# Attention over channels, then a gated layer: tokens in chunks of 1024 with 512-column products

## The chip, the cores and the metric

The kernel runs on one core of one Trainium2 chip. The metric is the device time of one execution in microseconds (us). Three runs of the kernel before took 2254.05 to 2256.57 us, with a median of 2255.52 us.

## The reference

For each of 4 batches, `q`, `k` and `v` are 6080 tokens by 256 channels in float32. Columns are normalised over the tokens, a 256x256 softmax over channels is formed, and `v` times that goes through two projections with a gate between them.

```python
qn = q / (np.linalg.norm(q, axis=1, keepdims=True) + 1e-06)
kn = k / (np.linalg.norm(k, axis=1, keepdims=True) + 1e-06)
s = kn.transpose(0, 2, 1) @ qn / tau
s = s - s.max(-1, keepdims=True)
a = np.exp(s)
a /= a.sum(-1, keepdims=True) + 1e-09
x = (v @ a).reshape(24320, 256)          # 4 batches of 6080 tokens
h = x @ w_in                             # 256 -> 2048
g = h * (1.0 / (1.0 + np.exp(-1.702 * h)))
return g @ w_out                         # 2048 -> 256
```

## The kernel before, in words

The softmax matrix and `w_in` are multiplied into one 256x2048 weight for each batch, so that the hidden layer is one product of `v` with that weight. All operands of TensorE are split into a high part and the rest (`split`, lines 81 to 84: ACT casts the high part, DVE subtracts), and a product is three matmuls: high by high, high by rest, rest by high.

**Tiling.** The 16 slices of 128 hidden columns are taken in pairs (`fp`, 8 of them). A chunk is 512 tokens (line 65); a batch has 11 chunks of 512 and one of 448. For one chunk and one pair the work is a 2x2 block product (two slices, two halves of the tokens, and a contraction over two halves of the 256 channels), done with seven products in place of eight: sums of blocks of `v` (`v_sums`, POOL) and of the weight (`weight_sums`) are made beforehand, and sums of products afterwards. In the kernel before a token half is 256 columns (224 in the last chunk), so each of these 21 matmuls is 256 columns wide.

**One pair** (`Hidden`, lines 530 to 596). `begin` makes products 0 and 4, copies one to SBUF (ACT, line 561) and adds it to the other (DVE, line 562). `middle` makes two more with two DVE additions (lines 569 and 571). `end` makes three with two additions (lines 577 and 578); then `gate` runs twice, over 512 columns each: an activation on ACT (line 589), and the split into `gh` and `gl`. PSUM has eight banks: four in `ps_h` (two sets of `ps_x` and `ps_y`), two in `ps_o` for the sums of the second projection, and two in `ps_s` for the scores of the next batch.

**The second projection** (`project`, line 600) adds six matmuls of 512 columns (line 610) for each of the two slices to the two banks of the chunk. After slice 15 the banks are copied out (lines 618 and 620).

**Order.** TensorE's order is written by hand (line 770): `begin` of a pair, `end` of the one before, a projection, work beside it, `middle`, a projection, work beside it. There are 192 such half steps in a batch, and a table of them (`put`) says at which one the work beside is emitted: the loads of the next batch's `q` and `k` and their split (`prepare`), its scores (line 299: four matmuls of 512 columns for each two token tiles; line 308: four of 256), its norms and softmax, its weights, and the next chunk's `v` (`v_load`, `v_sums`, `v_split`). The other engines are ordered by a planner when the program is built; work marked `pinned` is issued after the newest copy of line 561. A tile whose pool has no free buffer waits for the last reader of an old one. In the first steps of batch 0 the weights still have to be converted from 64-bit words, and two chunks run in turns (line 777). From `WIDE` on, the buffers of that conversion serve as more room for `gh` and `gl` (line 591).

Of the kernel before, what the change touches and what calls it, by code (L numbers as in the profile page):

```python
# [27 lines left out]
def channel_attention_then_glu(  # L28
# [35 lines left out]
    RT = 4  # L64
    chunks = [(o, min(NCH, N - o)) for o in range(0, N, NCH)]
    NCHUNK = len(chunks)

    const = ctx.enter_context(tc.tile_pool(name="const", bufs=1))
# [87 lines left out]
    def win_convert(n):  # L156
        g, c = divmod(n, NC2)
        if g not in win:
            win[g] = sp.tile([P, NC2, GW], F32, tag="win", name="win", bufs=1)
        yield from to_float32(win[g][:, c, :], words.pop(("in", n)), [P, GW])  # L160
# [17 lines left out]
    class Attention:  # L178
        def __init__(self, b, direct=0):
            self.b = b  # L180

            self.direct = direct
            self.alone = b == 0
            self.raw = {}
            self.firsts = {}

            short = UT if self.alone else 0
            self.rt = 6 if self.alone else RT
            self.loads = [(t, self.rt) for t in range(short, T + 1, self.rt)]
            if short:  # L190
                self.loads.insert(0, (0, short))
            self.wh = [None] * NG
            self.wl = [None] * NG

            self.units = [(t, min(UT, T - t)) for t in range(0, T, UT)]
            if TAIL:
                self.units.append((T, 1))

        def load(self, t0, room):
# [5 lines left out]
            tiles = {}  # L205
            for a, z in zip(cuts, cuts[1:]):
                for src, tag in ((q, "raw_q"), (k, "raw_k")):
                    if tag not in tiles:
                        if self.alone:
                            n = (t0 + self.rt - 1) // self.rt % NG  # L210
                            as_tag = {"raw_q": "wh", "raw_k": "wl"}[tag] + str(n)
                            tiles[tag] = wp.tile([P, self.rt, C], F32, tag=as_tag, name=tag)
                        else:
# [42 lines left out]

        def score_first(self, n):


            ps = ps_o.tile([P, NCH], F32, tag="o", name="s_first")  # L260
            todo = [(u, j, i) for u in range(self.direct) for j in range(UT) for i in range(NC2)]
            for m, (u, j, i) in enumerate(todo):
                rq, rk = self.fetched(u)
                nc.tensor.matmul(
                    ps[:, i * C : (i + 1) * C],
                    lhsT=rk[:, j, i * P : (i + 1) * P],
                    rhs=rq[:, j, :],
                    start=m == 0, stop=m == len(todo) - 1,
                    skip_group_check=True,
                )  # L270
# [3 lines left out]
            self.x = small.tile([P, NC2, C], F32, tag="x", name="x")  # L274
            nc.scalar.copy(self.x, ps.rearrange("p (c x) -> p c x", c=NC2))

        def score(self, u, qs, ks):
            nt = self.units[u][1]
            start = 0 if self.alone else self.direct
            if u == start:  # L280
                self.s = [
                    ps_s.tile([P, 2 * C], F32, tag=f"s{i}", name=f"s{i}")
                    for i in range(NC2)
                ]
            steps = [(j, i) for j in range(nt) for i in range(NC2)]
            last = u == len(self.units) - 1
            if u < self.direct:
                for j, i in steps:
                    nc.tensor.matmul(  # L289
                        self.s[i][:, :C],  # L290
                        lhsT=ks[:, j, i * P : (i + 1) * P],
                        rhs=qs[:, j, :],
                        start=u == start and j == 0,
                        stop=last and j == nt - 1,
                    )
                return

            for j, i in steps:
                nc.tensor.matmul(  # L299
                    self.s[i],  # L300
                    lhsT=ks[:, j, 0, i * P : (i + 1) * P],
                    rhs=qs[:, j, :, :],
                    start=u == start and j == 0,
                    stop=False,
                    skip_group_check=True,
                )
            for j, i in steps:
                nc.tensor.matmul(  # L308
                    self.s[i][:, C:],
                    lhsT=ks[:, j, 1, i * P : (i + 1) * P],  # L310
                    rhs=qs[:, j, 0, :],
                    start=False,
                    stop=last and j == nt - 1,
                    skip_group_check=True,
                )

        def norms_a(self, meanwhile=None):

            assert UT == 2
            ps = ps_h.tile([P, NCH], F32, tag="h", name="ps_n")  # L320
# [26 lines left out]
        def norms_c(self):  # L347

            ps = ps_h.tile([P, NCH], F32, tag="h", name="ps_b")
# [8 lines left out]
        def softmax_a(self, meanwhile=None):  # L358
            begun = not self.alone and self.direct
            if not begun:  # L360
                self.x = small.tile([P, NC2, C], F32, tag="x", name="x")
            self.z = small.tile([P, NC2], F32, tag="z", name="z")
            m = small.tile([P, NC2], F32, tag="m", name="m")
            for i in range(NC2):
                x, z, mi = self.x[:, i, :], self.z[:, i : i + 1], m[:, i : i + 1]
                s = self.s[i][:, :C]
                if not self.alone:
                    if begun:
                        nc.vector.tensor_tensor(x, self.s[i][:, C:], x, op=ALU.add)
                    else:  # L370
                        nc.scalar.copy(x, self.s[i][:, C:])
                    nc.vector.tensor_tensor(x, s, x, op=ALU.add)
                    s = x
                nc.vector.scalar_tensor_tensor(
                    x, in0=s, scalar=self.rn[:, NC2 + i : NC2 + i + 1], in1=self.rq,
# [24 lines left out]
        def spare(self, i, name):  # L400

            if self.alone:
                return ps_h.tile([P, NCH], F32, tag="h", name=name)
            return ps_s.tile([P, NCH], F32, tag=f"s{i}", name=name)

        def transposes(self, meanwhile=None):
            self.aT_h = small.tile([P, NC2, C], F32R, tag="aT_h", name="aT_h")
            self.aT_l = small.tile([P, NC2, C], F32R, tag="aT_l", name="aT_l")
            ps = self.spare(0, "ps_t")
# [12 lines left out]
        def win_load(self, g):  # L422

            win[g] = sp.tile([P, NC2, GW], F32, tag="win", name="win", bufs=1)
            nc.sync.dma_start(win[g], parts[g])

        def win_split(self, g, step=split):
            self.win_h = sp.tile([P, NC2, GW], F32R, tag="qs", name="win_h")
            self.win_l = sp.tile([P, NC2, GW], F32R, tag="ks", name="win_l")
            if self.alone:  # L430
                parts[g] = dram.tile([P, NC2, GW], F32, name=f"win{g}")
                nc.sync.dma_start(parts[g], win[g])
            return step(self.win_h, self.win_l, win[g])

        def weights(self, g, i):
# [7 lines left out]
            ps = self.spare(i, "ps_w")  # L443
# [14 lines left out]
            for f in range(2):  # L458
                nc.scalar.copy(self.wf[0][:, ((0, 3), (1, 2))[i][f]], src[:, f])  # L459
# [27 lines left out]
    def v_load(b, c):  # L487
# [3 lines left out]
        hw = w // 2  # L491

        early = b == 0 and c < 2
        room = [(wp, f"{t}{1 + c}") if early else (cv, "words") for t in ("wh", "wl")]
        t, u = (
            pool.tile([P, n, NCH // 2], F32, tag=tag, name="v_raw")
            for n, (pool, tag) in zip((4, 3), room)
        )
        vraw[b, c] = (t, u)
        src = vT[b, :, o : o + w].rearrange("(c p) (h n) -> p c h n", p=P, h=2)  # L500
        nc.sync.dma_start(t[:, 1:3, :hw], src[:, 1])
        nc.sync.dma_start(t[:, 0, :hw], src[:, 0, 0])
        nc.sync.dma_start(t[:, 3, :hw], src[:, 0, 1])

    def v_sums(b, c):

        hw = chunks[c][1] // 2
        t, u = (x[:, :, :hw] for x in vraw[b, c])
        eng = nc.gpsimd
        eng.tensor_tensor(u[:, 1], t[:, 2], t[:, 3], op=ALU.subtract)  # L510
        eng.tensor_tensor(t[:, 3], t[:, 3], t[:, 0], op=ALU.subtract)
        eng.tensor_tensor(u[:, 0], t[:, 2], t[:, 3], op=ALU.subtract)
        eng.tensor_tensor(u[:, 2], t[:, 1], u[:, 0], op=ALU.subtract)

    def v_split(b, c, part, step=split):

        hw = chunks[c][1] // 2
        if part == 0:
            vparts[b, c] = [
                vp.tile([P, 7, NCH // 2], F32R, tag=t, name=t) for t in ("vh", "vl")  # L520
            ]
        n = 4 if b == 0 and c < 2 else 2
        o = slice(2 * part, min(2 * part + n, 7))
        i = slice(2 * part % 4, 2 * part % 4 + (o.stop - o.start))
        h, l = (x[:, o, :hw] for x in vparts[b, c])
        return step(h, l, vraw[b, c][part // 2][:, i, :hw])

    wide = [0]

    class Hidden:  # L530
# [3 lines left out]
        def __init__(self, at, b, c, fp):  # L534
# [3 lines left out]
            self.v = vparts[b, c]  # L538

        def product(self, out, wi, vi, first=False, last=False):  # L540
            (wh, wl), (vh, vl) = self.w, self.v
            for n, (l, r) in enumerate(((wh, vh), (wh, vl), (wl, vh))):
                nc.tensor.matmul(  # L543
                    out, lhsT=l[:, wi, :], rhs=r[:, vi, : self.hw],
                    start=first and n == 0, stop=last and n == 2,
# [3 lines left out]
        def begin(self):  # L549
            hw = self.hw  # L550
            x, y = (ps_h.tile([P, NCH], F32, tag="h", name=nm) for nm in ("ps_x", "ps_y"))
            self.x = x[:, : 2 * hw].rearrange("p (h n) -> p h n", h=2)
            self.y = y[:, : 2 * hw].rearrange("p (h n) -> p h n", h=2)
# [338 lines left out]
```

## Time and profile before

| | |
|---|---|
| three runs, median (lowest to highest) | 2255.52 us (2254.05 to 2256.57) |
| profiled execution, first to last instruction (span) | 2252.1 us |
| TensorE (PE) busy, of the span | 2226.4 us, 99% |
| VectorE (DVE) busy | 1685.4 us, 75% |
| ScalarE (ACT) busy | 1339.5 us, 59% |
| GpSimd (POOL) busy | 446.3 us, 20% |
| mean granted TensorE clock | 0.999 |
| the chain that ended last | PE 91%, DVE 5%, ACT 2% |

Matmuls are pipelined, so the record of one lasts longer than the time until the next can start. What a matmul takes of TensorE's time is read from the starts of consecutive rows of the timeline.

### The profile page before, as it was taken

The page shows a single profiled execution, that of the slowest core. Times are in us where ns is not written, and L with a number is a line of the kernel's source. Part 1 is how long each engine was busy: PE and PEld are TensorE (multiplying, and loading weights), DVE is VectorE, ACT ScalarE, POOL GpSimd, SP SyncE. Part 2 cuts the span into 40 slices and gives each one's busy share as a digit, 9 for nine tenths or more (in the row PEclk, how much of TensorE's full clock was granted, in tenths as well). Part 3 has the DMA queues.
Part 4 walks back from the last instruction along what each step waited for, and adds up shares of the span by engine and source line. Part 5 has one row for each costly group of instructions (what it writes and reads, how often), then busy time and mean ns, then how long its engine had stood idle before and what let it go on. Part 6 is the DMA issues. An engine that isn't in the chain of part 4 may idle for free.

```text
span 2252.1 us, 36953 instructions
## 1 busy us (share of the span) xinstructions
PE 2226.4 (99%) x13712; PEld 1999.4 (89%) x13712; DVE 1685.4 (75%) x3346; ACT 1339.5 (59%) x2714; POOL 446.3 (20%) x420
## 2 busy tenths in 40 slices
PE   9899999999999999999999999999999999999999
PEld 8678888889989898988989999998898999999998
DVE  7988888776777878876677877877667666666665
ACT  7676666555666666655565666665556555555554
POOL 1024332210122323320022233331012101001000
PEclk9999999999999999999999999999999999999999
DMA  9222222100111212110010212110001000000000
GB/s 339 98 85 76 66 68 62 48 20 28 48 37 57 66 57 81 59 38 29 28 48 28 66 57 84 57 36 29 20 28 47 28 29 20 29 29 20 29 18 19
DMA packets 55205, 118.78 MB, mean 53 GB/s; under 512 B 6128, under 2 KB 20976, under 8 KB 55024
## 3 DMA queue, kind: packets, MB, share of 16 engines
q1 hardware_dynamic: 55024, 116.42, 15.9%
q8 instruction: 107, 1.75, 0.3%
q14 instruction: 74, 0.61, 0.1%
HBM read 89.39 MB, written 27.00 MB: 52 GB/s over the span
## 4 chain that ended last, share of the span: by engine, by line
PE 91%; DVE 5%; ACT 2%; issue 1%; DMA 1%; SPq 0%; DVEq 0%; ACTq 0%
PE ps_o L610 44%; PE ps_x L543 23%; PE ps_y L543 17%; PE s L299 3%; PE ps_w L452 2%; PE s L308 1%; PE s L289 1%; DVE wl L83 1%; DVE gl L83 0%; DVE win_l L83 0%; DVE u L562 0%; DMA raw_k<-in_k 0%; DVE z L133 0%; ACT wf L459 0%; DMA words<-in_w_in 0%
## 5 line engine op out<-in xcount | busy, mean ns | idle before, releaser
L83 DVE TENSOR_TENSOR gl<-g,gh 128x512 fp32r<-128x512 f32 (+1 forms) x768 | 568.8, 750 | 243.9 <-ACT gh L82 241.8
L610 PE MATMUL ps_o<-gl,wo_h 128*128 128x512 f32 (+1 forms) x1536 | 603.3, 393 | 0.9 <-DVE gl L83 0.9
L610 PE MATMUL ps_o<-gh,wo_h 128*128 128x512 f32 (+1 forms) x1536 | 604.2, 393 | 0.0
L610 PE MATMUL ps_o<-gh,wo_l 128*128 128x512 f32 (+1 forms) x1536 | 594.8, 387 | 0.0
L589 ACT ACTIVATE g<-ps_x 128x512 f32<-128x512 f32 (+1 forms) x384 | 227.2, 592 | 370.0 <-DVE ps_x L577 365.8
L82 ACT CAST gh<-g 128x512 fp32r<-128x512 f32 (+1 forms) x768 | 436.8, 623 | 1.0
L543 PE MATMUL ps_x<-vh,wh 128*128 128x256 f32 (+1 forms) x1536 | 433.3, 282 | 1.1 <-DVE r L569 1.1
L543 PE MATMUL ps_x<-vh,wl 128*128 128x256 f32 (+1 forms) x1536 | 433.8, 282 | 0.0
L543 PE MATMUL ps_x<-vl,wh 128*128 128x256 f32 (+1 forms) x1536 | 433.7, 282 | 0.0
L561 ACT COPY r<-ps_x 128x256 f32<-128x256 f32 (+1 forms) x384 | 142.7, 372 | 414.5 <-PE ps_x L543 414.3
L610 PEld LDWEIGHTS ps_o<-gh,wo_l 128*128 128x128 f32 x1536 | 288.7, 188 | 62.5
L543 PE MATMUL ps_y<-vh,wh 128*128 128x256 f32 (+1 forms) x1152 | 327.9, 285 | 12.3 <-DVE u L562 6.2
L543 PE MATMUL ps_y<-vh,wl 128*128 128x256 f32 (+1 forms) x1152 | 325.7, 283 | 1.9 <-DVE wl L83 1.9
L543 PE MATMUL ps_y<-vl,wh 128*128 128x256 f32 (+1 forms) x1152 | 325.3, 282 | 0.0
L610 PEld LDWEIGHTS ps_o<-gh,wo_h 128*128 128x128 f32 x1536 | 291.5, 190 | 34.6
L610 PEld LDWEIGHTS ps_o<-gl,wo_h 128*128 128x128 f32 x1536 | 291.5, 190 | 31.5 <-DVE gl L83 1.8
L543 PEld LDWEIGHTS ps_x<-vh,wh 128*128 128x128 f32 x1536 | 293.5, 191 | 16.2 <-DVE r L569 1.9
L543 PEld LDWEIGHTS ps_x<-vl,wh 128*128 128x128 f32 x1536 | 293.6, 191 | 12.5
L543 PEld LDWEIGHTS ps_x<-vh,wl 128*128 128x128 f32 x1536 | 293.8, 191 | 0.2 <-DVE wl L83 0.2
L562 DVE TENSOR_TENSOR u<-ps_y,r 128x256 f32<-128x256 f32 (+1 forms) x384 | 160.8, 419 | 139.0 <-ACT r L561 129.8
L543 PEld LDWEIGHTS ps_y<-vh,wh 128*128 128x128 f32 x1152 | 219.7, 191 | 36.1 <-DVE u L562 12.1
L569 DVE TENSOR_TENSOR r<-ps_x,u 128x256 f32<-128x256 f32 (+1 forms) x384 | 159.6, 416 | 121.4 <-PE ps_x L543 121.4
(119 smaller groups left out, 2991.2 us busy)
## 6 DMA issues: line engine op xcount, KB each, us to landing
out_T<-osb SPq DMA_DIRECT2D x88, 256.0 KB, 2.3
raw_q<-in_q SPq DMA_DIRECT2D x33, 512.0 KB, 3.6
raw_k<-in_k SPq DMA_DIRECT2D x33, 512.0 KB, 4.5
v_raw<-in_vT SPq DMA_DIRECT2D x44, 256.0 KB, 2.8
v_raw<-in_vT SPq DMA_DIRECT2D x88, 128.0 KB, 2.9
win<-win SPq DMA_DIRECT2D x16, 512.0 KB, 3.2
raw_q<-in_q SPq DMA_DIRECT2D x6, 768.0 KB, 8.9
raw_k<-in_k SPq DMA_DIRECT2D x6, 768.0 KB, 10.2
```

What stands on the lines that cost most here:

```text
L82: ins = nc.scalar.copy(dst_hi, src)
L83: nc.vector.tensor_tensor(dst_lo, src, dst_hi.bitcast(F32), op=ALU.subtract)
L289: nc.tensor.matmul(self.s[i][:, :C], lhsT=ks[:, j, i * P : (i + 1) * P], rhs=qs[:, j, :], start=u == start and j == 0, stop=last and j == ...
L299: nc.tensor.matmul(self.s[i], lhsT=ks[:, j, 0, i * P : (i + 1) * P], rhs=qs[:, j, :, :], start=u == start and j == 0, stop=False, skip_gro ...
L308: nc.tensor.matmul(self.s[i][:, C:], lhsT=ks[:, j, 1, i * P : (i + 1) * P], rhs=qs[:, j, 0, :], start=False, stop=last and j == nt - 1, sk ...
L452: nc.tensor.matmul(ps, lhsT=l[:, j, ci], rhs=r[:, j, :], start=n == 0, stop=n == 3 * NC2 - 1,)
L543: nc.tensor.matmul(out, lhsT=l[:, wi, :], rhs=r[:, vi, : self.hw], start=first and n == 0, stop=last and n == 2, skip_group_check=True,)
L561: newest[0] = nc.scalar.copy(r1, self.x[:, 0])
L562: nc.vector.tensor_tensor(u2, self.y[:, 1], r1, op=ALU.add)
L569: nc.vector.tensor_tensor(r, self.x[:, 1], self.u2, op=ALU.add)
L589: nc.scalar.activation(g, ps, AF.Gelu_apprx_sigmoid)
L610: nc.tensor.matmul(out[d][:, :w], lhsT=l[:, f, ds], rhs=r[:, :w], start=f == 0 and n == 0, stop=f == NF - 1 and n == 2,)
```

## The change

A chunk becomes 1024 tokens, and a half of it 512 columns (the last chunk of a batch has 960, so 480), in the same seven products. One pair now takes three banks (`a`, `b`, `c`, each single), the second projection four (`o0` to `o3`, two for each half), and the scores one (`s`). A pair is four steps (`slot` 0 to 3), with one projection of the pair in step 3 and the other three in steps 0 to 2 of the next pair. There are again 192 steps in a batch. Three results are copied from PSUM to SBUF by ACT and three DVE additions follow; one of the four gated blocks is gated in SBUF. The pair of buffers for `gh` and `gl` goes from three to two, with two more from `WIDE` on. Scores of the next batch go into one bank, by three matmuls of 256 columns where there was one of 512 and one of 256. The split `w_in` is kept in DRAM in both parts and loaded again, where it was split again. `q` and `k` of a later batch are loaded two token tiles at a time (before: four).

```diff
-    chunks = [(o, min(NCH, N - o)) for o in range(0, N, NCH)]
+    WCH = 2 * NCH
+    chunks = [(o, min(WCH, N - o)) for o in range(0, N, WCH)]
-    vp = ctx.enter_context(tc.tile_pool(name="vp", bufs=2))
-    gp = ctx.enter_context(tc.tile_pool(name="gp", bufs=3))
+    vp = ctx.enter_context(tc.tile_pool(name="vp", bufs=1))
+    gp = ctx.enter_context(tc.tile_pool(name="gp", bufs=2))
-    ps_h = ctx.enter_context(tc.tile_pool(name="ps_h", bufs=4, space=PSUM))
-    ps_o = ctx.enter_context(tc.tile_pool(name="ps_o", bufs=2, space=PSUM))
+    ps_h = ctx.enter_context(tc.tile_pool(name="ps_h", bufs=1, space=PSUM))
+    ps_o = ctx.enter_context(tc.tile_pool(name="ps_o", bufs=1, space=PSUM))
+    def bank(tag, name):
+        pool = {"a": ps_h, "b": ps_h, "c": ps_h, "s": ps_s}.get(tag, ps_o)
+        return pool.tile([P, NCH], F32, tag=tag, name=name)
...
             for j, i in steps:
+                ci = slice(i * P, (i + 1) * P)
+                self.product(i, ks[:, j, 0, ci], qs[:, j, 0, :])
+                self.product(i, ks[:, j, 0, ci], qs[:, j, 1, :])
+                self.product(i, ks[:, j, 1, ci], qs[:, j, 0, :], last and j == nt - 1)
...
         def win_load(self, g):
-            win[g] = sp.tile([P, NC2, GW], F32, tag="win", name="win", bufs=1)
-            nc.sync.dma_start(win[g], parts[g])
+            for t, part in zip((self.win_h, self.win_l), parts[g]):
+                nc.sync.dma_start(t.bitcast(F32), part)
...
+    V_ROOM = {"px": (2, 2), "py": (2, 2), "pz": (2, 1), "pw": (1, 1)}
...
+        def copied(self, src):
+            r = gp.tile([P, NCH], F32, tag="r", name="r", bufs=3)[:, : self.hw]
+            newest[0] = nc.scalar.copy(r, src)
+            return r
+
+        def slot(self, k):
             hw = self.hw
+            if k == 0:
+                self.z = bank("c", "ps_z")[:, :hw]
+                self.product(self.z, 3, 3, first=True)
+                self.r5 = self.copied(self.z)
+                self.x = bank("a", "ps_x")[:, :hw]
+                self.product(self.x, 0, 0, first=True)
+                r1 = self.copied(self.x)
+                y = bank("b", "ps_y")[:, :hw]
+                self.product(y, 1, 1, first=True, last=True)
+                nc.vector.tensor_tensor(y, y, r1, op=ALU.add)
+                self.gate(0, 0, y)
+            elif k == 1:
+                self.product(self.x, 4, 4)
+                self.r2 = self.copied(self.x)
+            elif k == 2:
+                self.product(self.x, 5, 5)
+                nc.vector.tensor_tensor(self.r5, self.x, self.r5, op=ALU.add)
+                self.product(self.z, 6, 2, last=True)
+                nc.vector.tensor_tensor(self.z, self.z, self.r2, op=ALU.add)
+                self.gate(0, 1, self.z)
+                self.gate(1, 1, self.r5)
+            else:
+                self.product(self.x, 2, 6, last=True)
+                self.gate(1, 0, self.x)
...
-            there = wide[0] and wide[0] % 5 < 2
+            there = wide[0] and gates[0] % 2
+            gates[0] += 1
             pool, tags = (cv, ("z", "low")) if there else (gp, ("gh", "gl"))
...
-                    at_u = first + 4 * (u - nd)
+                    at_u = first + 5 * (u - nd)
                     put(at_u - 4, nxt.fetched, u)
                     put(at_u, pinned, prep, u)
                     put(at_u + 3, score, u)
-                e = first + 4 + 4 * (nu - nd)
+                e = between(first + 4 + 5 * (nu - nd))
                 put(e, nxt.norms_a)
-                put(e + 9, nxt.norms_c)
-                put(e + 10, nxt.softmax_a)
-                put(e + 16, nxt.transposes)
+                put(e + 4, nxt.norms_c)
+                put(e + 5, nxt.softmax_a)
+                put(e + 8, nxt.transposes)
...
+            for s in range(total):
+                at_slot = s % SLOTS
+                if at_slot == 0:
+                    h = Hidden(at, b, *divmod(s // SLOTS, NF // 2))
+                h.slot(at_slot)
+                if at_slot == 3:
+                    h.project(0, 0)
+                elif before is not None:
+                    before.project(*((0, 1), (1, 0), (1, 1))[at_slot])
+                for fn, a in side.get(s, ()):
+                    fn(*a)
+                if at_slot == 3:
+                    before = h
```

## Rows read from the trace of the kernel before

**Rows 1.** The profile's page: span, and busy time of each engine (part 1).

```profile
span 2252.1 us, 36953 instructions
...
PE 2226.4 (99%) x13712; PEld 1999.4 (89%) x13712; DVE 1685.4 (75%) x3346; ACT 1339.5 (59%) x2714; POOL 446.3 (20%) x420
```

**Rows 2.** Busy time by stretch: from:to, length, then each engine's busy us.

```profile
0.00:180.00 180.00, 161.59 (x858) 138.17 (x859) 153.87 (x289) 126.77 (x234) 40.11 (x45) 0.99 0.48 169
...
1800.00:2252.00 452.00, 448.14 (x2817) 405.94 (x2815) 298.66 (x647) 233.63 (x477) 29.32 (x36) 1.00 0.07 24
```

**Rows 3.** TensorE's waits after 180 us: releaser, total us, times, longest; the largest.

```profile
PE ps_y L543 <- DVE u L562: 1.8, 10, 0.2
```

**Rows 4.** TensorE's waits before 180 us: the one with the longest single wait.

```profile
PE ps_y L543 <- DVE u L562: 4.4, 2, 3.0
```

**Rows 5.** Timeline of TensorE in batch 1: start, record's length, line, tiles, shape.

```profile
799.80 0.28 PE L543 MATMUL ps_x<-vh,wh 128*128 128x256 f32 x1
...
801.60 0.40 PE L610 MATMUL ps_o<-gh,wo_h 128*128 128x512 f32 x1
801.83 0.40 PE L610 MATMUL ps_o<-gl,wo_h 128*128 128x512 f32 x1
802.07 0.39 PE L610 MATMUL ps_o<-gh,wo_l 128*128 128x512 f32 x1
...
802.99 0.28 PE L543 MATMUL ps_y<-vh,wh 128*128 128x256 f32 x1
...
803.70 0.40 PE L610 MATMUL ps_o<-gh,wo_h 128*128 128x512 f32 x1
```

**Rows 6.** The same view: the scores of two token tiles, and what follows.

```profile
840.92 1.07 PE L299 MATMUL s<-qs,ks 128*128 128x512 f32 x4
841.83 0.64 PE L308 MATMUL s<-qs,ks 128*128 128x256 f32 x4
842.30 0.28 PE L543 MATMUL ps_x<-vh,wh 128*128 128x256 f32 x1
```

**Rows 7.** The same view in the last chunk: a projection of 448 columns, products of 224.

```profile
2215.11 0.37 PE L610 MATMUL ps_o<-gh,wo_h 128*128 128x448 f32 x1
...
2216.33 0.27 PE L543 MATMUL ps_y<-vh,wh 128*128 128x224 f32 x1
...
2216.99 0.38 PE L610 MATMUL ps_o<-gh,wo_h 128*128 128x448 f32 x1
```

**Rows 8.** Groups by shape: one part of the products into `ps_x`; count, busy us, mean ns.

```profile
L543 PE MATMUL ps_x<-vh,wh 128*128 128x256 f32 x1408 | 398.6, 283 | 1.1 <-DVE r L569 1.1
```

**Rows 9.** Groups by shape on ACT and DVE: count, busy us, mean ns of one.

```profile
L83 DVE TENSOR_TENSOR gl<-g,gh 128x512 fp32r<-128x512 f32 x704 | 527.2, 758 | 220.3 <-ACT gh L82 218.5
L82 ACT CAST gh<-g 128x512 fp32r<-128x512 f32 x704 | 403.4, 627 | 0.8
...
L589 ACT ACTIVATE g<-ps_y 128x512 f32<-128x512 f32 x352 | 208.7, 593 | 1.5 <-DVE ps_y L578 1.5
L577 DVE TENSOR_TENSOR ps_x<-ps_x,u 128x256 f32<-128x256 f32 x352 | 150.2, 427 | 19.5 <-PE ps_x L543 16.4
...
L561 ACT COPY r<-ps_x 128x256 f32<-128x256 f32 x352 | 131.4, 373 | 395.3 <-PE ps_x L543 395.3
...
L83 DVE TENSOR_TENSOR ks<-raw_k,ks 128x512 fp32r<-128x512 f32 x65 | 106.4, 1637 | 0.0
...
L618 DVE COPY osb<-ps_o 128x512 f32<-128x512 f32 x44 | 30.1, 683 | 0.0
...
L620 ACT COPY osb<-ps_o 128x512 f32<-128x512 f32 x44 | 25.8, 587 | 54.4 <-PE ps_o L610 54.4
```

**Rows 10.** Timeline of ACT around one softmax: table load, and the next copy.

```profile
474.83 1.28 ACT L388 ACT_TABLE_LOAD   x1
...
479.68 0.35 ACT L561 COPY r<-ps_x 128x256 f32<-128x256 f32 x1
```

**Rows 11.** The profile's page: loads of `k`, KB each, median us to landing.

```profile
raw_k<-in_k SPq DMA_DIRECT2D x33, 512.0 KB, 4.5
```

More of the change, by code (lines that the diff above doesn't have):

```diff
@@ L188, in __init__ @@
             self.rt = 6 if self.alone else RT
-            self.loads = [(t, self.rt) for t in range(short, T + 1, self.rt)]
+            self.early = ["px", "py"][: direct * UT // 4] if not self.alone else []
+            begun = short + 4 * len(self.early)
+            self.loads = [(4 * n, 4) for n in range(len(self.early))]
+            self.loads += [(t, self.rt) for t in range(begun, T + 1, self.rt)]
             if short:
@@ L273, in score_first @@
             yield
-            self.x = small.tile([P, NC2, C], F32, tag="x", name="x")
-            nc.scalar.copy(self.x, ps.rearrange("p (c x) -> p c x", c=NC2))
         def score(self, u, qs, ks):
             nt = self.units[u][1]
[L279 to L284, printed above, removed]
+            if u == 0:
+                self.start_scores("o3" if self.alone else "s")
             steps = [(j, i) for j in range(nt) for i in range(NC2)]
@@ L288, in score @@
                 for j, i in steps:
[L289 to L294, printed above, removed]
+                    self.product(
+                        i, ks[:, j, i * P : (i + 1) * P], qs[:, j, :], last and j == nt - 1
                     )
@@ L298, in score @@
             for j, i in steps:
[L299 to L315, printed above, removed]
+                ci = slice(i * P, (i + 1) * P)
+                self.product(i, ks[:, j, 0, ci], qs[:, j, 0, :])
+                self.product(i, ks[:, j, 0, ci], qs[:, j, 1, :])
+                self.product(i, ks[:, j, 1, ci], qs[:, j, 0, :], last and j == nt - 1)
         def norms_a(self, meanwhile=None):
             assert UT == 2
[L320 removed]
+            ps = bank("b", "ps_n")
             for n in range(2 * NC2):
@@ L347, in norms_c @@
         def norms_c(self):
-            ps = ps_h.tile([P, NCH], F32, tag="h", name="ps_b")
+            ps = bank("c" if self.alone else "b", "ps_b")
             for i in range(NC2):
@@ L442, in weights @@
                 ]
-            ps = self.spare(i, "ps_w")
+            ps = bank("ac"[i] if self.alone and g == 0 else "b", "ps_w")
             ci = slice(i * P, (i + 1) * P)
@@ L505, in v_sums @@
[L505 to L526, printed above, removed]
@@ L530, in channel_attention_then_glu, with v_split @@
+    def v_split(b, c, tag, step=split):
+        hw = chunks[c][1] // 2
+        n, bufs = V_ROOM[tag]
+        h, l = (
+            vp.tile([P, n, NCH], F32R, tag=f"{tag}_{t}", name=f"v{t}", bufs=bufs) for t in "hl"
+        )
+        vparts[b, c, tag] = h, l
+        x, y = vraw[b, c, tag in ("pz", "pw")]
+        src = {"px": x, "py": y, "pz": y, "pw": x[:, 1:, :]}[tag]
+        return step(h[:, :, :hw], l[:, :, :hw], src[:, :, :hw])
+    wide = [False]
+    gates = [0]
     class Hidden:
```

328 lines of the change are left out of this document (149 added, 179 removed).

## The prediction

> **What bounds the kernel now.** I read the busy times of the page first, then the stretches, then TensorE's waits, and last its timeline. TensorE is busy for 2226.4 of 2252.1 us, no other engine for more than 1685.4 [rows 1]. Of the 25.7 us in which it is idle, 18.4 lie in the first 180 us [rows 2]; after that its largest wait sums to 1.8 us in ten pieces [rows 3]. So behind the start the kernel is one row of matmuls without gaps, and only what a matmul takes of TensorE's time, and the number of matmuls, set the end. Busy time doesn't tell that: the record of a 256-column matmul lasts 0.28 us and of a 512-column one 0.40, and they overlap [rows 5]. The starts tell it. Fifteen matmuls of 256 columns run from 799.80 to 801.60, six more from 802.99 to 803.70: 21 in 2.51 us, 0.1195 each. Six of 512 columns run from 801.60 to 802.99: 0.2317 each [rows 5]. Two of 256 take 0.239, one of 512 takes 0.2317: twice the width costs less than twice the time.
>
> **The products.** Before, a pair of slices of one chunk has 21 product matmuls. 4 batches x 12 chunks x 8 pairs x 21 = 8064, of which 32 x 21 = 672 are in the last chunks and 7392 are 256 wide (the group of 1408 is one of the three parts of the four products into one tile: 11 chunks x 8 x 4 x 4) [rows 8]. In the last chunks six of 224 columns run from 2216.33 to 2216.99, 0.110 each, and six of 448 from 2215.11 to 2216.33, 0.2033 each [rows 7]. Sum: 7392 x 0.1195 + 672 x 0.110 = 957.2 us. After, there are 4 x 6 x 8 x 21 = 4032, 3360 of 512 columns and 672 of 480. No 512-wide product is in the trace. The nearest rows are the projections: the same three matmuls (the first two with one weight, the streamed operand changing from high part to rest and back), 0.2317. At 480 columns I go halfway between 0.2033 and 0.2317, 0.2175. Sum: 3360 x 0.2317 + 672 x 0.2175 = 924.7, a gain of **32.5 us**. The bounds: the scores' four matmuls of 512 take 0.91 us, 0.2275 each [rows 6], where one streamed operand serves two weights; with that (0.2133 at 480) the gain is 49.5. The longest interval among the projections is 0.24, from 801.83 to 802.07 [rows 5]; if every product took that (0.2258 at 480), the sum would be 958.1 and the gain nothing. I take the projections' mean because the operands follow each other in the same way.
>
> **The projections** keep their six matmuls per slice and half. Before, 4224 of them are 512 wide and 384 are 448 wide: 978.7 + 78.1 = 1056.8 us; after, 3840 and 768 of 480: 889.7 + 167.0 = 1056.7. Nothing.
>
> **The scores.** Before, four of 512 in 0.91 us and four of 256 in 0.47 [rows 6] for two token tiles. After, twelve of 256: 12 x 0.1175 = 1.41, or 1.43 at the products' 0.1195. That is 0.03 to 0.05 us more for each of 68 such units (272 matmuls of line 299 in all, four to a unit): **+3 us**, on the path, since TensorE has no gaps.
>
> **ACT and DVE.** For 1024 tokens and one pair ACT loses two copies of 256 columns (0.373) and gains three of 512 from PSUM (0.587, the copy of line 620): +1.0 us x 192 = +195 on 1339.5, near 68% of the span. DVE loses ten additions of 256 (0.427) and gets three of 512 (0.683, the copy of line 618, is the nearest row): -2.2 x 192 = -425 on 1685.4 [rows 1, 9]. Neither engine becomes the bound; both costs are hidden by TensorE as long as no chain through them is longer than TensorE's way round. The work that `w_in`'s second split took from both goes as well.
>
> **The chains in a pair, with single banks.** A product takes 0.70 us and a projection 1.39, a pair 45 x 0.2317 = 10.43. From the start of step 0: z to 0.70, x to 1.39, y to 2.09, projection to 3.48, x again to 4.17, projection to 5.56, x again to 6.26, z again to 6.95, projection to 8.34, x a last time to 9.04, projection to 10.43. A result is there about 0.2 us later (a record of 0.39 against an interval of 0.23, and the next engine). Three waits are new. (1) Step 2 adds to x, so the copy r2 has to be done: 4.37 + 0.59 = 4.96 against 5.56, a margin of 0.6. (2) Step 3 adds to x, so DVE's r5 has to be done: 6.46 + 0.69 = 7.15 against 8.34, a margin of 1.2. (3) The next pair starts bank `a` at 11.13, so the activation of x has to be done. ACT gets z at 7.15 + 0.69 = 7.84; two activations (0.593) and two casts (0.627), whose starts are about 0.5 apart, end at 9.9; the activation of x ends at 10.5: a margin of 0.6. Behind a late r2 on ACT stand the gate of z and r5, and behind TensorE's wait for it everything else, the projections too. Work beside the pair can take the margins: on DVE one subtraction for `ks` lasts 1.64 us on average [rows 9], 0.4 more than margin (2); on ACT a softmax with its table loads keeps the copy waiting from 474.83 to 479.68 [rows 10], 4.85 us with two casts among them, three times. I count up to 3 us for each softmax, and 0.1 us for about half of the 140 pairs that have work beside them: 0 to 25 us, of which I take **+10**.
>
> **The start.** TensorE's longest wait in the early part, 3.0 us for DVE's addition of line 562 [rows 4], goes: the same bank's next product now waits for a copy on ACT alone, which doesn't stand behind DVE's weight splits. DVE, busy for 153.9 of 180 us there [rows 2], gets 2.2 us of each 10 back. Against that, `gh` and `gl` have two pairs of buffers for the 6.5 pairs until `WIDE`: the cast of x must wait for the projection of z (3.48), and cast 0.63, subtraction 0.76 and two handovers end at 5.1 where its own projection would start at 4.17, 0.9 us a pair. What is late next is y's projection. -8 to +12, taken as **0**.
>
> **Queues.** SP issues two loads of `w_in` parts per weight group in place of one and loads of `q` and `k` twice as often, half as large; each stands four or more steps of 2.6 us ahead of its use, and a 512 KB load lands in 4.5 us [rows 11]. POOL's sums take as many elements as before. I cost these at nothing; the cover gone, each late load stops the row of matmuls for what it lacks.
>
> **The sum.** On the profiled execution: 2252.1 - 32.5 + 3 + 10 + 0 = 2232.6; the median lies 3.4 us above that execution's span, which I keep: **2236 us**. Its own range: best 49.5 gained, 3 paid, no stalls and 8 saved at the start, near 2201; worst 32.5 gained with 25 of stalls, 2251. I call 2207 to 2251 its range.
>
> **The rivals.** (A) The single banks cost more than the width gives. For: three banks where two sets of two stood, margins of 0.6 us, and ACT 9 points busier, in strict order. Against: DVE has 20 points less to do, and the trace shows no waits with DVE at 75%. The price: if the 140 pairs with work beside lose the 0.44 us by which a `ks` subtraction overruns margin (2), 62 us in place of 10, 2288 us. It turns to slower where stalls pass 30 us, 0.16 us a pair of all 192. (B) The start: two pairs of buffers cost 0.9 us for x and as much for y over 6.5 pairs, 12 us, 2248. (C) The width gives next to nothing, because the part of a matmul beyond its columns isn't one per instruction but grows with the width: it is 0.24 for some projections, and at that price for all products the time is 2236 + 32.5 = 2268; at 0.2365 about 2256. For it speaks that the projections' intervals are uneven, 0.23 and 0.24 [rows 5], with the same order of operands; against it that the mean over six is 0.2317. The Trainium skill's page "TensorE: Matmul & The Clock Gate", section "Wait — 56ns, not 53.3ns?", puts that fixed part at about 2.5 ns for each matmul and the whole of a 512-column one at 215.7 ns, by which halving 4032 pairs of matmuls would save only 10 us, and C would hold. The trace does not agree: two of 256 less one of 512 is 7 to 11 ns by its rows.
>
> **How the numbers follow.** Forecast 0.58; A 0.17; B 0.13; C 0.10; 0.02 that stalls at the start vanish and products run at the scores' pace, below 2207. A measurement can tell about 0.2%, 4.5 us, so the bounds are 2251 and 2260. The forecast is faster; B is 0.11 faster and 0.02 within; C 0.01 faster, 0.05 within, 0.04 slower; A 0.01 within and 0.16 slower. Faster 0.72, same 0.08, slower 0.20. The range 2207 to 2266 leaves out most of A and the low tail.
>
> **What would show it.** In the trace after: six 512-column product matmuls from start to start in 1.39 us (1.365 is the better bound, 1.44 is C); TensorE's matmul rows fewer by about 3760 (4032 products less, 272 scores more); ACT near 68% busy, DVE near 56%. Waits of products into ps_x for ACT's copy r or its g above 30 us in sum are A; waits of line 610's successor for gl before about 140 us are B. The forecast goes wrong above all if ACT's order, made by the planner from its own times, puts work beside ahead of r2 or of the gate of x.

## The result, and the profile after

| | before | changed |
|---|---|---|
| median | 2255.38 us | 2230.68 us |
| lowest to highest of four runs | 2254.05 to 2256.57 | 2229.19 to 2231.76 |
| ratio of the changed kernel to the one before, 95% interval | | 0.9892 (0.9878 to 0.9906) |
| profiled execution's span | 2252.1 us | 2228.8 us |

The change gained 24.7 us, 1.1%; 19.5 were forecast. That the sum came out near is luck: the matmuls gained more than forecast and the stalls cost more, by some 30 us each.

The page of the changed kernel, span and busy times (part 1), against [rows 1]:

```profile
span 2228.8 us, 27422 instructions
...
PE 2174.7 (98%) x9952; PEld 1806.7 (81%) x9952; DVE 1321.5 (59%) x1894; ACT 1568.5 (70%) x2769; POOL 428.8 (19%) x348
```

TensorE's records are 3760 fewer, 13712 to 9952, the number forecast. ACT is at 70% and DVE at 59%, near the 68 and 56 that were worked out. TensorE's idle time has doubled, from 25.7 to 54.1 us. The stretches say where (from:to, length, busy us of PE, PEld, DVE, ACT and POOL with counts, granted clock, DMA share, GB/s), against [rows 2]:

```profile
0.00:180.00 180.00, 156.92 (x650) 122.96 (x651) 142.63 (x227) 131.28 (x228) 36.08 (x37) 0.97 0.50 181
180.00:2228.00 2048.00, 2017.75 (x9304) 1683.71 (x9302) 1178.85 (x1668) 1437.22 (x2542) 392.68 (x311) 1.00 0.18 58
```

In the first 180 us it is idle for 23.1 us (before: 18.4), behind them, to the end of the span, for 31.0 (before: 7.3). TensorE's waits of the changed kernel after 180 us (waiting engine, tile and line, releaser: us in total, times, longest), where the one before had nothing over 1.8 us in sum [rows 3]:

```profile
PE ps_o L604 <- DVE gl L90: 11.9, 12, 1.5
PE ps_x L540 <- ACT r L548: 7.1, 6, 2.1
PE ps_x L540 <- DVE r L569: 5.3, 5, 1.7
```

And before 180 us, the largest three, where the largest of before was 4.4 us for DVE's `u` [rows 4]:

```profile
PE ps_o L604 <- DVE gl L90: 5.8, 7, 2.4
PE ps_w L444 <- ACT g L585: 3.4, 2, 3.2
PE ps_o L604 <- ACT gh L89: 2.6, 3, 1.8
```

What paid for this is seen in the starts on TensorE's timeline (start, record's length, line, tiles, shape), against [rows 5]; first one product of 512 columns and one projection, then in the last chunk a product of 480, then the scores of two token tiles and the six products behind them:

```profile
1951.85 0.39 PE L540 MATMUL ps_z<-vh,wh 128*128 128x512 f32 x1
...
1952.53 0.39 PE L604 MATMUL ps_o<-gh,wo_h 128*128 128x512 f32 x1
...
1953.89 0.39 PE L540 MATMUL ps_x<-vh,wh 128*128 128x512 f32 x1
...
2160.50 0.37 PE L540 MATMUL ps_z<-vh,wh 128*128 128x480 f32 x1
...
2161.15 0.38 PE L540 MATMUL ps_x<-vh,wh 128*128 128x480 f32 x1
...
727.16 1.59 PE L275 MATMUL s<-qs,ks 128*128 128x256 f32 x12
728.60 0.40 PE L540 MATMUL ps_x<-vh,wh 128*128 128x512 f32 x1
...
729.98 0.39 PE L604 MATMUL ps_o<-gh,wo_h 128*128 128x512 f32 x1
```

Three product matmuls of 512 columns take 0.68 us, 0.2267 each, and six projection matmuls 1.36, also 0.2267: the projections, which the change leaves as they are, were at 0.2317 before. A product matmul of 480 takes 0.2167 (0.65 for three). The twelve score matmuls take 1.44 us, against 1.38 before [rows 6].

Put together by these rows: the products go from 957.2 us to 3360 x 0.2267 + 672 x 0.2167 = 907.3, a gain of 50; the projections gain about 3840 x 0.005 = 19; the scores lose 68 x 0.06 = 4. With no more stalls than before, the span would be 2252.1 - 50 - 19 + 4 = 2187 us. The 42 us from there to 2228.8 are new stalls: 28 of them show as idle time. Of the rest, stretches at the lower clock make up some 5 us, an estimate from the mean granted clock (0.997, before 0.999); what is left should be pauses that a matmul's record hides.

These intervals are from quiet stretches. Over all starts of the two traces, without the intervals that a stall stretches by more than a quarter, the means are 0.2277 for a product and 0.2272 for a projection (before: 0.2312). By them the products gain about 46 us, the projections about 17, and the new stalls are about 35.

### The profile page after: what moved, and what is told of

It is laid out like the page before. It is cut to its first block, busy times and chain, and to the rows that moved or that the text cites. A ratio compares the mean times of both kernels' runs of the same rounds, so it can differ in the third digit from the quotient of the medians.

```text
span 2228.8 us, 27422 instructions
## 1 busy us (share of the span) xinstructions
PE 2174.7 (98%) x9952; PEld 1806.7 (81%) x9952; DVE 1321.5 (59%) x1894; ACT 1568.5 (70%) x2769; POOL 428.8 (19%) x348
## 5 line engine op out<-in xcount | busy, mean ns | idle before, releaser
L90 DVE TENSOR_TENSOR gl<-g,gh 128x512 fp32r<-128x512 f32 (+1 forms) x576 | 431.4, 755 | 334.3 <-ACT gh L89 334.3
L500 POOL TENSOR_TENSOR v_raw<-v_raw 128x512 f32<-128x512 f32 (+1 forms) x120 | 168.4, 1404 | 803.5 <-DMA v_raw<-in_vT 724.5
L540 PE MATMUL ps_x<-vh,wh 128*128 128x512 f32 (+1 forms) x768 | 301.9, 393 | 15.2 <-ACT r L548 7.8
L540 PE MATMUL ps_x<-vl,wh 128*128 128x512 f32 (+1 forms) x768 | 298.5, 389 | 0.0
L540 PE MATMUL ps_x<-vh,wl 128*128 128x512 f32 (+1 forms) x768 | 298.0, 388 | 0.0
L548 ACT COPY r<-ps_x 128x512 f32<-128x512 f32 (+1 forms) x384 | 224.7, 585 | 37.0 <-PE ps_x L540 23.4
L562 DVE TENSOR_TENSOR ps_y<-ps_y,r 128x512 f32<-128x512 f32 (+1 forms) x192 | 133.0, 693 | 171.5 <-PE ps_y L540 167.8
L90 DVE TENSOR_TENSOR gl<-r,gh 128x512 fp32r<-128x512 f32 (+1 forms) x192 | 143.1, 745 | 153.6 <-ACT gh L89 153.0
L540 PEld LDWEIGHTS ps_x<-vh,wh 128*128 128x128 f32 x768 | 144.6, 188 | 51.9 <-DVE r L569 12.3
L540 PEld LDWEIGHTS ps_x<-vh,wl 128*128 128x128 f32 x768 | 144.3, 188 | 29.5
```

Of the source, the lines that this page charges most:

```text
L90: nc.vector.tensor_tensor(dst_lo, src, dst_hi.bitcast(F32), op=ALU.subtract)
L500: nc.gpsimd.tensor_tensor(out, a, z, op=ALU.subtract)
L540: nc.tensor.matmul(out, lhsT=l[:, wi, :], rhs=r[:, n, : self.hw], start=first and m == 0, stop=last and m == 2, skip_group_check=True,)
L548: newest[0] = nc.scalar.copy(r, src)
L562: nc.vector.tensor_tensor(y, y, r1, op=ALU.add)
```

## Experiments

Each kernel here was timed beside the kernel before, whose median lay between 2254.9 and 2255.4 us every time; so they are set beside the changed kernel's 2230.7 us.

### The width alone: products as two matmuls of 256 columns

```diff
-                nc.tensor.matmul(
-                    out, lhsT=l[:, wi, :], rhs=r[:, n, : self.hw],
+                for a in (0, self.hw // 2):
+                    cs = slice(a, a + self.hw // 2)
+                    nc.tensor.matmul(
+                        out[:, cs], lhsT=l[:, wi, :], rhs=r[:, n, cs],
```

> The changed kernel with each product matmul of 512 columns made as two of 256 with the same weight; banks, order and all else as changed. Theory W (the width itself gives the gain): two of 256 take 0.239 us by the rows of before, one of 512 starts 0.227 after the last in the changed kernel, so 4032 x 0.012 = 48 us are given back. Theory P (in addition, a 512-wide projection matmul takes 0.2317 behind 256-wide products and 0.227 behind 512-wide ones): its intervals go back to about 0.2317, 4608 x 0.0045 = 21 us more. Up to 35 us of the changed kernel's stalls can hide behind a slower TensorE. W alone: 2245 to 2279 us; W and P: 2265 to 2300 us, slower than before. Rival F (the gain per matmul is a small fixed cost, and the rest of the gain came from the new banks and order): about 2241 us.

The kernel so edited loses part of the product sums (how is not shown), but it issues the matmuls that are to be compared: 13984, that is 4032 more. Measured: 2280.2 us, ratio to before 1.0108 (1.0093 to 1.0123), 49.5 us slower than the changed kernel. Its timeline:

```profile
1952.49 0.40 PE L542 MATMUL ps_x<-vh,wh 128*128 128x256 f32 x2
...
1953.93 0.40 PE L606 MATMUL ps_o<-gh,wo_h 128*128 128x512 f32 x1
...
1955.32 0.40 PE L542 MATMUL ps_x<-vh,wh 128*128 128x256 f32 x2
```

Twelve products of 256 take 1.44 us, 0.12 each, and the six projection matmuls behind them 1.39 us again, 0.2317. So both parts hold: the products' width is worth about 45 to 50 us, and a projection matmul is 0.005 us slower behind narrow matmuls than behind wide ones. The sum of the two, 60 to 70 us, shows as 50, at least in part because a slower TensorE waits less (its idle time is 45.5 us, from a span of 2279.1 and 2233.6 busy, 8.6 less than in the changed kernel). With the new banks and order but the old width the change loses to the kernel before. The theory of a small fixed cost, 2241 us, falls.

### A third pair of buffers at the start

```diff
             pool, tags = (cv, ("z", "low")) if there else (gp, ("gh", "gl"))
+            if not wide[0] and gates[0] % 3 == 0:
+                pool, tags = op, ("osb", "osb")
```

> The changed kernel with a third pair of buffers for gh and gl in the steps before WIDE (the two output buffers, idle there). Theory B (two pairs of buffers are what TensorE waits for in the first 180 us): its waits for gl and gh there, 8.4 us, fall below 3, and the time by 5 to 10 us, to 2221 to 2226. Rival S (the waits come from the conversions of the weights queued ahead on ACT and DVE): within 3 us of the changed kernel.

Measured: 2220.3 us (2215.8 to 2224.8), 10.4 less than the changed kernel. Its stretch and two of its waits before 180 us:

```profile
0.00:180.00 180.00, 163.00 (x693) 129.67 (x694) 150.86 (x238) 139.40 (x244) 40.58 (x41) 0.99 0.53 191
...
PE ps_w L444 <- ACT g L585: 3.5, 2, 3.2
...
PE ps_o L606 <- DVE gl L90: 1.1, 1, 1.1
```

The waits for `gl` and `gh`, 8.4 us, are down to 1.1, the idle time from 23.1 to 17.0, and the granted clock of the stretch is up from 0.97 to 0.99. Two pairs, with the gates in this order, are what TensorE waited for, as theory B has it; the gain is a little over its 5 to 10 us. The wait of the weights' product (`ps_w`) for bank `b` stays.

### Without POOL's sums of squares

```diff
-                    eng = nc.vector if self.alone else nc.gpsimd
-                    eng.tensor_tensor(acc, acc, sq, op=ALU.add)
+                    if self.alone:
+                        nc.vector.tensor_tensor(acc, acc, sq, op=ALU.add)
```

> The changed kernel without POOL's sums of squares of q and k in batches 1 to 3 (the norms are then those of the first tiles alone; their squares on ACT stay). Theory C (DVE's subtractions last up to 1.76 us because POOL adds at the same time, and that makes r5 and gl late): the ks subtraction goes from 0.906 us on average to about 0.75, TensorE's waits for DVE after 180 us, 17.2 us, fall below 6, and the time by 8 to 14 us, to 2217 to 2223. Rival O (what is late is late because of the order in DVE's queue): waits for gl stay near 11.9 us, time within 5 us of the changed kernel.

Measured: 2214.2 us, 16.5 less. After 180 us:

```profile
PE ps_o L604 <- DVE gl L90: 8.3, 9, 1.5
...
PE ps_x L540 <- DVE r L569: 2.4, 5, 0.8
```

The time is even below what C expects, but the waits for DVE fell from 17.2 to 10.7 us, not below 6, and the `ks` subtraction from 0.906 to 0.791 us. POOL's sums of squares explain about half of r5's lateness and a third of `gl`'s. The rest of the gain lies elsewhere, part of it in the first 180 us (idle for 20.0 us there; granted clock 0.99), where these additions run as well. Part of it is the clock: these rows are from an execution of 2210.0 us with a mean granted clock of 0.999, and the other three took 2214.1 to 2214.5 with 0.995 to 0.997. Neither theory holds by itself.

The edit leaves POOL's sums of `v` in place. In the changed kernel they run beside DVE's subtractions at a wait for z's `gl` (start, length, engine, line; the wait in brackets):

```profile
609.15 1.22 DVE L90 TENSOR_TENSOR vl<-v_raw,vh 128x1024 fp32r<-128x1024 f32 x1
...
610.21 1.30 POOL L500 TENSOR_TENSOR v_raw<-v_raw 128x512 f32<-128x512 f32 x1 [9.48 <-DMA v_raw<-in_vT]
...
610.28 1.74 DVE L90 TENSOR_TENSOR gl<-r,gh 128x480 fp32r<-128x480 f32 x1
...
611.94 1.21 DVE L90 TENSOR_TENSOR gl<-g,gh 128x480 fp32r<-128x480 f32 x2
...
612.65 0.48 PE L604 MATMUL ps_o<-gl,wo_h 128*128 128x480 f32 x1 [1.47 <-DVE gl L90]
```

One `gl` subtraction takes 1.74 us beside POOL's, and the two behind it 1.21 together. In each of the changed kernel's ten waits for z's `gl` after 180 us, one subtraction of 1.69 to 1.83 us stands so. That POOL's sums of `v` cause part of these waits is not shown: no run takes them away.

### The gate of r5 last

```diff
                 self.gate(0, 1, self.z)
-                self.gate(1, 1, self.r5)
             else:
                 self.product(self.x, 2, 6, last=True)
                 self.gate(1, 0, self.x)
+                self.gate(1, 1, self.r5)
```

> The changed kernel with the gate of r5 emitted last in the pair, behind that of x (its projection is the last of the four). Theory O (gl of z is late since DVE and ACT take r5's cast and subtraction first): TensorE's waits for gl after 180 us fall from 11.9 us to under 4, the time by 6 to 12 us, to 2219 to 2225. Rival C (they are late because DVE is slowed by POOL): waits for gl stay above 8 us, time within 3 us of the changed kernel.

Measured: 2228.5 us, 2.2 less. After 180 us:

```profile
PE ps_x L540 <- DVE r L569: 9.9, 8, 1.9
PE ps_o L604 <- DVE gl L90: 8.1, 10, 1.3
```

The waits for `gl` fell by 3.8 us and those for r5 rose by 4.6. The order moves DVE's lateness from one reader to the other; it doesn't remove it. Theory O falls as stated; the rival's figures came (above 8 us, within 3 us), though the run before this one shows that POOL's sums of squares are only part of it. Before 180 us the waits for `gl` and `gh` fell from 8.4 to 2.3 us, with two pairs of buffers as before; the time shows little of that, at a mean granted clock of 0.994 in the profiled execution, where the changed kernel had 0.997.

### Without the softmax's table loads

```diff
-                nc.scalar.activation(x, x, AF.Exp, bias=mi, accum_out=z)
+                nc.scalar.activation(x, x, AF.Gelu_apprx_sigmoid if self.b else AF.Exp, bias=mi, accum_out=z)
```

> The changed kernel with the gate's activation in place of the exponential in the softmax of batches 1 to 3 (another function of the same size), so that ACT's two table loads at each softmax go. Theory T (the copy r2 stands behind the table loads on ACT, and TensorE behind r2): the waits for ACT's copy r after 180 us, 7.1 us, fall below 2, and with the half-clock stretch behind the one at 1084 us the time falls by 5 to 8 us, to 2222 to 2226. Rival (that copy is late because of other work on ACT): waits for r stay near 6 us and the time within 2 us of the changed kernel.

Measured: 2222.2 us, 8.5 less. The waits for ACT's copy went from 7.1 to 1.0 us:

```profile
PE ps_x L540 <- DVE r L569: 8.1, 7, 1.7
...
PE ps_x L540 <- ACT r L548: 1.0, 2, 0.5
```

Theory T holds. The waits for `gl` fell as well, to 7.9 us, while those for r5 rose from 5.3 to 8.1. ACT's timeline of the changed kernel at the softmax of batch 2 shows the queue: two table loads, two exponentials, a gate and its cast stand ahead of r2's copy, which TensorE needs for its next matmul.

```profile
1080.76 1.28 ACT L372 ACT_TABLE_LOAD   x1
...
1083.16 1.28 ACT L585 ACT_TABLE_LOAD   x1
1084.46 0.60 ACT L585 ACTIVATE g<-ps_y 128x512 f32<-128x512 f32 x1
...
1085.61 0.58 ACT L548 COPY r<-ps_x 128x512 f32<-128x512 f32 x1
```

### The split of q and k always in step 0

```diff
-                first = STEPS + 3 if b == 0 else 20
+                first = STEPS + 4 if b == 0 else 20
-                    at_u = first + 5 * (u - nd)
+                    at_u = first + 4 * (u - nd)
-                e = between(first + 4 + 5 * (nu - nd))
+                e = between(first + 4 + 4 * (nu - nd))
```

> The changed kernel with the split of q and k emitted every 4 steps, always in step 0, where it was every 5 and so in each step in turn. Theory M (step 0 leaves the q and k subtractions time before DVE's addition r5, which has 1.2 us to spare; in steps 1 to 3 they run into it): TensorE's waits for r5 after 180 us fall from 5.3 us to under 1.5 and its waits for gl from 11.9 to under 8; time lower by 4 to 10 us, 2221 to 2227. Rival (the v split and POOL cause these waits): time within 3 us of the changed kernel.

Measured: 2226.6 us, 4.1 less. The waits for r5 fell from 5.3 to 1.4 us, as theory M expects. Those for `gl` did not: 13.1 us, so something else makes them.

### Three edits together

The third pair, step 0 for q and k, and the softmax one pair later in step 1, behind r2's copy:

```diff
-                put(e + 5, nxt.softmax_a)
-                put(e + 7, nxt.softmax_c)
-                put(e + 8, nxt.transposes)
+                put(e + 7, pinned, nxt.softmax_a)
+                put(e + 9, nxt.softmax_c)
+                put(e + 10, nxt.transposes)
```

> The changed kernel with the third pair of buffers at the start, the split of q and k in step 0, and the softmax emitted in step 1 behind the copy r2 (norms and transposes accordingly). If the stalls add up, it gains 10 (third pair, measured) + 4 to 10 (step 0) + 2 to 5 (softmax): 2206 to 2215 us. If they are one queue of work that only shifts: 2216 to 2222.

Measured: 2211.0 us, 19.7 less, ratio to before 0.9804 (0.9787 to 0.9820). The gains add up: 10.4 and 4.1 us for the two edits timed alone leave 5.2 for the softmax's move, which was not timed alone. After 180 us all its waits are these:

```profile
PE ps_o L606 <- DVE gl L90: 12.1, 14, 1.3
PE ps_x L540 <- ACT g L585: 0.8, 3, 0.3
PE ps_x L540 <- DVE r L569: 0.7, 3, 0.2
```

With the waits for r5 and r2 gone, I tried the order of the gates once more on top of this (the same edit as above).

> The kernel with the third pair, the split of q and k in step 0 and the softmax in step 1 (2211.0 us measured), and in addition the gate of r5 emitted behind that of x. With r5's waits gone (0.7 us after 180 us), theory O once more: the 12.1 us of waits for gl, which lie where two v splits and the subtraction for r5 stand ahead of z's on DVE, fall to 5 to 8 us (one 0.6 us subtraction less in each of about ten): 2204 to 2209 us. Rival: the order moves other work ahead instead, as it did alone (waits for r5 up by 4.6 us, for gl down by 3.8): 2209 to 2214 us.

Measured: 2215.6 us, 4.6 more than without it, above both expectations; `gl` stays at 12.4 us. The order of z's and r5's gates is not the cause of `gl`.

### The two wide splits of v apart

Rows of ACT, DVE and TensorE in the kernel with three edits, at one of the waits for `gl`:

```profile
681.04 2.02 ACT L89 CAST vh<-v_raw 128x1024 fp32r<-128x1024 f32 x2
...
682.90 1.22 DVE L90 TENSOR_TENSOR vl<-v_raw,vh 128x1024 fp32r<-128x1024 f32 x1
682.94 0.64 ACT L89 CAST gh<-g 128x512 fp32r<-128x512 f32 x1
...
684.03 0.69 DVE L571 TENSOR_TENSOR ps_z<-ps_z,r 128x512 f32<-128x512 f32 x1
...
684.63 1.22 DVE L90 TENSOR_TENSOR vl<-v_raw,vh 128x1024 fp32r<-128x1024 f32 x1
...
685.76 0.69 DVE L90 TENSOR_TENSOR gl<-g,gh 128x512 fp32r<-128x512 f32 x1
...
686.50 0.50 PE L606 MATMUL ps_o<-gl,wo_h 128*128 128x512 f32 x1 [1.31 <-DVE gl L90]
```

Both 1024-column splits of the next chunk's `v` stand in one pair: they are emitted at steps 21 and 23 of the chunk, both in the pair of steps 20 to 23, and both are pinned behind the same copy r2. TensorE is in step 3 here, whose projection reads y's `gl`. On ACT the cast for it (682.94) stands behind the two casts of `v`; on DVE the subtraction (685.76) stands behind both splits and z's addition. Of the 14 waits for `gl`, the eight long ones, 10.3 of 12.1 us, are such waits for y's `gl`, one in a chunk; the other six, 1.7 us, are for z's. In the changed kernel it is the other way round: ten of its twelve, 9.3 of 11.9 us, are for z's and two for y's. All of them come from the pair of steps 20 to 23.

```diff
-                put(n - (5 if late else 9), pinned, v_split, *bc, "px")
-                put(n - (4 if late else 7), v_load, *bc, True)
-                put(n - (3 if late else 5), pinned, v_sums, *bc, True)
+                put(n - (5 if late else 7), pinned, v_split, *bc, "px")
+                put(n - (4 if late else 6), v_load, *bc, True)
+                put(n - (3 if late else 4), pinned, v_sums, *bc, True)
```

> The kernel with the third pair, the split of q and k in step 0 and the softmax in step 1 (2211.0 us), and in addition the two 1024-column splits of the next chunk's v no longer in one pair but in two (the second two steps later, the load behind it one step later). Theory V (the two v splits, 1.22 us each on DVE within 3 us, make gl late at one step of each chunk): the waits for gl after 180 us fall from 12.1 us to under 4 and the time by 5 to 9 us, 2202 to 2206 us. Rival (gl is late because z's addition, its gate and its split follow each other too closely, with or without v): waits above 9 us, time 2209 to 2213 us.

Measured: 2189.8 us, ratio to before 0.9710 (0.9694 to 0.9727), 21.2 less than with three edits. The only wait left on TensorE after 180 us, and the stretch:

```profile
PE ps_x L540 <- ACT g L585: 0.8, 3, 0.3
...
180.00:2187.00 2007.00, 2001.22 (x9266) 1678.03 (x9264) 1151.49 (x1659) 1415.51 (x2531) 392.82 (x309) 1.00 0.18 58
```

Theory V holds, and gave more than the 12.1 us of waits: TensorE's idle time fell from 37.3 to 24.1 us and its busy time from 2172.3 to 2163.8. With the same 9952 matmuls and the same mean granted clock, 0.998, the busy time that went should be pauses inside records: at the wait above, two matmuls take 2.03 us (684.81 to 686.84), 1.58 more than two of 0.2267, for 1.31 us of idle time. The edit also moves the second load of `v` and POOL's sums behind it by one step, and that was not tried apart from the split. The span, 2187.9 us, is near the 2187 worked out above for the changed matmuls with the stalls of before, and the idle time, 24.1, near the 25.7 of before.

The same move on the changed kernel without the other edits:

> The changed kernel with the two 1024-column splits of v moved into two pairs, and nothing else. Theory V (they make gl late in each chunk; with the other three edits in place the move took 21 us): the waits for gl after 180 us fall from 11.9 us to under 3 and the time by 12 to 20 us, 2211 to 2219 us. Rival (alone, the split of q and k in all four steps takes the time that v leaves on DVE, and only the three edits together let it count): waits for gl at 6 us or more, time 2222 to 2228 us.

Measured: 2224.1 us, 6.6 less than the changed kernel.

```profile
PE ps_x L540 <- DVE r L569: 6.1, 8, 1.8
PE ps_o L604 <- DVE gl L90: 3.7, 8, 1.3
```

The waits for `gl` fell by 8.2 us, nearly as V expects; the time came out as in the rival. Some 5 us of the profiled execution, an estimate, are the clock: its mean was 0.994, where the changed kernel had 0.997. The move is worth 6.6 us alone and 21.2 beside the others. That the split of q and k, still in all four steps here, takes part of the room is what the waits for r5 suggest; how much of the difference it makes was not tried.

## Why the prediction was right, and where it was not

The median was 2230.7 us where 2236 were forecast. Most of the mechanism was right. The sizes of what the matmuls gain and of what the stalls cost were not, and that these errors cancelled is luck.

**What bounds the kernel**: right. The row of matmuls sets the end, and undoing the width alone turns the gain into a loss of 24.8 us against the kernel before.

**The products**: mechanism right, size off. The step took the projections' interval of 0.2317 as the nearest row; the products run at 0.2267, by the bound that the scores gave (49.5 us; by the rows it is 50, by the means 46). The reason for the choice, that the operands follow each other as in the projections, was not what sets the interval. What precedes is: with the same three operands the projections are at 0.2317 behind 256-column products and at 0.2267 behind 512-column ones, in two kernels that differ in that alone.

**The projections**, costed at nothing: wrong by 17 to 19 us, for the same reason. An operation that the change doesn't touch was costed by its row of before, though that row holds in its old company.

**The scores**: +3 forecast, +4 by the rows. **ACT and DVE**: 70 and 59% against 68 and 56, neither a bound.

**The chains**: the waits forecast for r2 and r5 came, with longest 2.1 and 1.7 us; the softmax was put at up to 3 us, and its table loads cost a wait of 2.1. The term of +10 us was mis-sized: idle time behind 180 us rose by 24 us, and the new stalls are 35 to 42 us in all. What the step left out is the largest sum of waits, 11.9 us for `gl`: 9.3 for z's on the next pair's first projection, 2.6 for y's on the pair's own. I had followed the banks through the pair, and not these chains from the addition over gate, cast and subtraction to the projection. In the one pair of a chunk where all these waits arise, `v` splits stand in front of them on DVE, and in z's waits a subtraction is slow beside POOL as well.

**The start**, taken as 0 between -8 and +12: its idle time rose by 4.7 us. The wait for DVE's `u` is gone, as said, and waits for `gl` and `gh` of 8.4 us have come in its place: rival B, shown by the third pair. Rival B was priced at 12 us; the pair gave 10.4.

**Rival A** was the right worry: new stalls of 35 to 42 us in place of about 10. Its sign did not come, though: the waits of products into `ps_x` for ACT's r or g sum to 7.3 us after 180 us, not to 30, and the larger part lies elsewhere. The stalls would have turned the result to slower, as its point of 30 us says, had the matmuls not given twice what was forecast. **Rival C** falls with the products' interval. The Trainium skill's page "TensorE: Matmul & The Clock Gate", section "Wait — 56ns, not 53.3ns?", puts the fixed part of a matmul at about 2.5 ns, by which halving 4032 pairs of matmuls would save some 10 us, an estimate from its figure. The trace does not agree: splitting them again cost 49.5 us.

## What to carry to other kernels

Where one engine's row of instructions is the bound, read what an instruction takes from start to start, and read it in the company that it will have after the change: the instructions in front of it set it too. When banks become single, follow each result to the end of its chain, up to the instruction that reads it in the next round, and look for wide work that is queued in front of any link, and for another engine's work beside which a link runs slower. Work beside the main row that is emitted at two steps can still land in one place if both are pinned to the same instruction; moving one of the two into the next pair was worth 21.2 us here beside the other edits, and 6.6 alone.

## What the runs showed of the hardware

Six 512-column matmuls took 1.39 us from start to start behind 256-column ones, 0.2317 each, and 1.36, 0.2267 each, behind 512-column ones. The changed kernel shows it within itself: the six products behind the scores' 256-column matmuls take 1.38 us (728.60 to 729.98). Why narrow matmuls leave the wider ones behind them slower is open.

A DVE subtraction of 128x480 took 1.74 us while POOL subtracted 128x512, and about 0.6 a piece right after.

A wait of TensorE can be followed by a cost beyond its length. Behind the 2.05 us wait for r2 at the softmax of batch 2, matmuls of the changed kernel start 0.42 us apart, at the 1.2 GHz level (granted clock 0.50 from 1087.10 to 1090.40), until 1090.44:

```profile
1086.24 0.50 PE L540 MATMUL ps_x<-vh,wh 128*128 128x512 f32 x1 [2.05 <-ACT r L548]
...
1087.04 0.62 PE L540 MATMUL ps_z<-vh,wh 128*128 128x512 f32 x1
1087.46 0.63 PE L540 MATMUL ps_z<-vl,wh 128*128 128x512 f32 x1
...
1090.44 0.41 PE L604 MATMUL ps_o<-gh,wo_l 128*128 128x512 f32 x1
...
1633.88 0.50 PE L540 MATMUL ps_x<-vh,wh 128*128 128x512 f32 x1 [2.05 <-ACT r L548]
```

Eight matmuls take 3.40 us there where 0.2267 each would make 1.81, so that 1.6 us came on top of the wait of 2.05. It need not: behind the equally long wait that ended at 1633.88, at the next softmax, the granted clock is 1.00 (1634.50 to 1638.00) and matmuls start 0.23 us apart.
